# Linear attention and a GELU block on one core: batch 1's preparation reordered between output tiles, and a narrower last store

## The chip, the cores and the metric

The kernel runs on one core of a Trainium2 chip. The metric is the device time of one execution in microseconds, the median over several runs. Profiles are of one execution, taken by the hardware profiler.

## The reference, cut to what matters

```python
# q, k, v: [8 batches, 8 heads, 576 positions, 64], f32
def phi(x): return np.where(x > 0, x, np.exp(x) - 1.0) + 1.0
q_p, k_p = phi(q), phi(k)
kv  = np.einsum('bhsd,bhse->bhde', k_p, v)
z   = np.sum(k_p, axis=2)
num = np.einsum('bhsd,bhde->bhse', q_p, kv)
den = np.einsum('bhsd,bhd->bhs', q_p, z)[..., None] + 1e-06
x   = (num / den) as [4608 tokens, 512]
h   = x @ w_in                       # [512, 2048]
g   = 0.5 * h * (1.0 + np.tanh(c * (h + 0.044715 * h**3)))
out = g @ w_out                      # [2048, 512], f32
```

So each batch is a small linear attention, whose result goes through two large matrix products with a GELU between them.

## The kernel before

**The large products.** Of each batch's 576 positions, 512 ("main") are one iteration `j` of the outer loop; the 64 that are left over from each of the eight batches are gathered into a ninth iteration (`j == B`, 8). An iteration multiplies the transposed attention result `xt` (bf16, 128 partitions x 4 blocks x 512 tokens) by `w_in`: 16 blocks `m` of four 512-column matmuls each (`h_mm`, L349), each block into one PSUM bank, and ScalarE's GELU (L359) takes the bank into `g`. Then four output tiles `t` of 128 tokens are accumulated over 16 matmuls each (`o_mm`, L642), evacuated by ScalarE or VectorE (`evac`, L608) and stored in pairs (L633). A "step" is one h block, or one quarter `u` (four matmuls) of one output tile.

**The order.** The schedule is written out by hand: instructions go to each engine in the order in which the Python code makes them, and each engine takes its own queue strictly in that order. `iteration` walks through the 32 steps ("slots") of an iteration and after each calls `run(j, slot)`, which issues whatever `at(j, slot, ...)` has put there. In iteration 0 the slots 0 to 15 are the h blocks, and 16 to 31 the output steps with `u` outermost: slot 24 is tile 0's third quarter, slot 28 tile 0's last quarter, slots 29, 30 and 31 the last quarters of tiles 1, 2 and 3. So all four output tiles hold a PSUM bank until the end. There are six banks in one rotating pool (`bank`), and one pair of banks (`pair_of_banks`).

**Batch 1's attention** (`plan_second`) lies in those output slots of iteration 0, so that iteration 1 can begin directly after:

- slot 15: phi of q and k (`maps`: ScalarE exponentials, VectorE linear parts and minima, and a part of the w_out cast)
- slot 23: q transposed by TensorE (L469)
- slot 25: v cast to bf16 in two halves (`cast_v_paired`, L241): VectorE one, ScalarE the other
- slot 26: the products `kv` (L263, 72 small matmuls in two halves, the second half on the second half of v), the evacuation into `kvbd` (L290) by VectorE and ScalarE, and the last quarter of w_out's cast (L143) by VectorE, ScalarE and GpSimd
- slots 27 to 30: for each of four chunks `c` of 128 tokens, `n(c)`: four 130-column matmuls (L294) that give numerator and denominator at once, and VectorE's reciprocal and product (`nab_evac`, L307 and L309), which write `x`
- slots 28 to 31: `t(c)`: `x` transposed by TensorE (L341) and copied by ScalarE into `xt` (L342)
- slots 30 and 31: `h_quarter`: the first two h blocks of iteration 1, chunk by chunk, 128 columns at a time

`nab` puts n into the pair of banks, so that the next n has to wait until VectorE has made x from the one before. `nab_in_banks` puts n into two single banks and evacuates them one after the other (L329, L330); the first batch, prepared before the loop, uses the two in turn.

**The first batch** (`first_batch`) also uses `h_quarter`, with three blocks. Batches 2 to 7 are prepared later, from `plan_prepare` and `plan_attention`, with transposes by DMA.

**The output tiles of iteration 0** (`finish`): each is evacuated as soon as its last quarter is issued, tiles 0, 1 and 2 by ScalarE and tile 3 by VectorE; the two stores wait until slot 2 of iteration 1.

**The end.** The last output tile of the ninth iteration (`last_tile`) is made in two halves of 256 columns, each accumulated over all 16 blocks, evacuated (the first by VectorE, the second by ScalarE) and stored in two DMAs of 64 rows, one issued by ScalarE and one by SyncE (`store_rest`, L613).

Of the kernel before, what the change touches and what calls it, by code (L numbers as in the profile page):

```python
# [15 lines left out]
def kernel(  # L16
# [15 lines left out]
    nc = tc.nc  # L32

    B, H, S, D = q.shape
    d_model, d_ff = moe_w_in.shape
    P = 128
    HP = P // 2
    C = 4
    MAIN = P * C
# [34 lines left out]
    def bank(name, shape, dt=FP32):  # L74
        return ps_b.tile(shape, dt, name=name, tag="b")

    def pair_of_banks(name):
        return ps_a.tile([P, 2, 512], FP32, name=name, tag="a")
# [63 lines left out]
    def cast_w_out(i, fn, ms=slice(0, 4)):  # L142
        fn(  # L143
            out=w_out_sb[:, 4 * i + ms.start : 4 * i + ms.stop, :],
            in_=w_st[False, i][:, ms],
        )

    nc.scalar.preload_act_table_set("exp_and_others")
    halves = (slice(0, 2), slice(2, 4))
# [40 lines left out]
    def vp_paired(b):  # L190
        return vps[b % 2].rearrange("p (j u) e -> p j u e", u=NP)
# [48 lines left out]
    def cast_v_paired(b, us, fn):  # L240
        fn(  # L241
            out=vp_paired(b)[:, :, us, 0:D].rearrange("p j u d -> p u j d"),
            in_=ld["v", b][:, us].rearrange("p u (j d) -> p u j d", d=D),
        )
# [72 lines left out]
    def nab(qt_c, b):  # L317
        n_ps = pair_of_banks("n_ps")
        nab_mm(qt_c, kvbds[b % 4], [n_ps[:, a] for a in range(2)])
        return nab_evac(n_ps, b in PAIRED)  # L320
# [23 lines left out]
    xts = {}  # L344
    qts = {}

    def h_mm(h_ps, xt, m, ts=slice(0, MAIN)):
        for c in range(KM):
            nc.tensor.matmul(  # L349
                h_ps[:, ts],  # L350
                lhsT=w_in_sb[:, c, P * m : P * (m + 1)],
                rhs=xt[:, c, ts],
                start=(c == 0),
                stop=(c == KM - 1),
                skip_group_check=True,
            )
# [3 lines left out]

    h_begun = {0: {}, 1: {}}

    def h_quarter(j, c, blocks):
        for m in range(blocks):
            if c == 0:
                h_begun[j][m] = bank("h_ps", [P, MAIN])
            h_mm(h_begun[j][m], xts[j], m, slice(P * c, P * (c + 1)))

    def xt_chunk(j, c):
        return xts[j][:, :, P * c : P * (c + 1)]  # L370
# [1 line left out]
    def gelu_table():  # L372
        nc.scalar.preload_act_table_set("gelu_apprx_tanh_and_others")  # L373
# [65 lines left out]
    fill = {}  # L439

    def at(j, slot, fn, *args):
        j, slot = j + slot // 32, slot % 32
        fill.setdefault((j, slot), []).append((fn, args))

    def run(j, slot):
        for fn, args in fill.get((j, slot), ()):
            fn(*args)

    def plan_second():
        b = 1  # L450
        x = {}

        def maps():
            for n in "qk":
                exp_of(n, b)
            gelu_table()
            for n in "qk":
                linear_of(n, b)
            least_of("q", b)
            cast_w_out(2, nc.vector.tensor_copy, slice(2, 4))  # L460
            least_of("k", b)

        def transpose_q():
            qts[b] = pt.tile([P, C, NP, P], BF16, name="qt")
            for s in range(2):
                t_ps = bank("t_ps", [P, 2, NP, P], BF16)
                for c in range(2):
                    for i in range(NP):
                        nc.tensor.transpose(  # L469
                            t_ps[:, c, i, :],  # L470
                            phi["q", b][:, 2 * s + c, 2 * i : 2 * i + 2, :],
                            ident,
                        )
                nc.scalar.copy(qts[b][:, 2 * s : 2 * s + 2], t_ps)

        def casts():
            cast_v_paired(b, halves[0], nc.vector.tensor_copy)
            cast_v_paired(b, halves[1], nc.scalar.copy)

        def kv():  # L480
            kv_ps = [bank("kv_ps", [P, 2, E]) for _ in range(2)]
            for ii in range(2):
                kv_paired(b, ii, lambda a, ii: kv_ps[a][:, ii, :])
            cast_w_out(3, nc.vector.tensor_copy, slice(0, 1))
            for a, fn in enumerate((nc.vector.tensor_copy, nc.scalar.copy)):
                kv_evac(b, slice(2 * a, 2 * a + 2), kv_ps[a], fn)

        def last_w_out():
            cast_w_out(3, nc.scalar.copy, slice(1, 2))
            cast_w_out(3, nc.gpsimd.tensor_copy, slice(2, 4))  # L490

        def n(c):
            x[c] = nab(qts[b][:, c], b)

        def t(c):
            if c == 0:
                xts[b] = pt.tile([P, NP, MAIN], BF16, name="xt")
            transpose_x(x[c], xt_chunk(b, c), nc.scalar.copy)

        at(0, 15, maps)  # L500
        at(0, 23, transpose_q)
        at(0, 25, casts)
        at(0, 26, kv)
        at(0, 26, last_w_out)
        at(0, 27, n, 0)
        at(0, 28, n, 1)
        at(0, 28, t, 0)
        at(0, 29, n, 2)
        at(0, 29, t, 1)
        at(0, 30, h_quarter, b, 0, 2)  # L510
        at(0, 30, n, 3)
        at(0, 30, t, 2)
        at(0, 31, h_quarter, b, 1, 2)
        at(0, 31, t, 3)
        at(0, 31, h_quarter, b, 2, 2)
        at(0, 31, h_quarter, b, 3, 2)

    def plan_prepare(b, s_linear, s_exp):
        rest = b % 2 == 0
# [87 lines left out]
    def evac(dst, src, on_scalar):  # L607
        (nc.scalar.copy if on_scalar else nc.vector.tensor_copy)(dst, src)  # L608
# [10 lines left out]
    def finish(j, t, o_ps):  # L619
        if j == B:  # L620
            o_sb = pout.tile([P, 2, d_model], FP32, name="o_sb")
            evac(o_sb[:, 0, :], o_ps, t % 2)
            store_rest(t, o_sb, slice(0, d_model), (nc.scalar, nc.sync))
            return
        if t % 2 == 0:
            o_sbs[j, t // 2] = pout.tile([P, 2, d_model], FP32, name="o_sb")
        o_sb = o_sbs[j, t // 2]
        evac(o_sb[:, t % 2, :], o_ps, t < C - 1 if j == 0 else t % 2)
        if t % 2 == 1:
            ov = out[j * S : j * S + MAIN, :].rearrange("(p c) f -> p c f", c=C)[:, t - 1 : t + 1]  # L630

            def store():
                nc.scalar.dma_start(out=ov, in_=o_sb)  # L633

            if j == 0:
                at(1, 2, store)
            else:
                store()

    def o_mm(o_ps, g, t, u, fs=slice(0, d_model)):  # L640
        for m in range(4 * u, 4 * u + 4):
            nc.tensor.matmul(  # L642
                o_ps,
                lhsT=g[:, m, P * t : P * (t + 1)],
                rhs=w_out_sb[:, m, fs],
                start=(m == 0),
                stop=(m == MM - 1),
            )

    def last_tile(g, t):  # L650
        hw = d_model // 2
        o_sb = pout.tile([P, 2, d_model], FP32, name="o_sb")
        for s in range(2):
            fs = slice(hw * s, hw * (s + 1))
            o_ps = bank("o_ps", [P, hw])
            for u in range(4):
                o_mm(o_ps, g, t, u, fs)
            evac(o_sb[:, 0, fs], o_ps, s)
            store_rest(t, o_sb, fs, (nc.scalar, nc.sync))

    def iteration(j):
        xt = xts[j] if j < B else xt_rest
        g = pg.tile([P, MM, MAIN], BF16, name="g")
        hs = [("h", m) for m in range(MM)]
        if j == 0:
            steps = hs + [("o", t, u) for u in range(4) for t in range(C)]
        elif j == 1:
            os = [[("o", t, u) for u in us for t in range(C)] for us in ((0, 1), (2, 3))]
            steps = hs[:8] + os[0] + hs[8:] + os[1]
        else:  # L670
            steps = hs + [("o", t, u) for t in range(C) for u in range(4)]
        o_pss = {}
        for slot, step in enumerate(steps):
            if step[0] == "h":
                m = step[1]
                h_ps = h_begun.get(j, {}).get(m)
                if h_ps is None:
                    h_ps = bank("h_ps", [P, MAIN])
                    h_mm(h_ps, xt, m)
                gelu(g, m, h_ps)  # L680
            else:
                t, u = step[1:]
                if j == B and t == C - 1:
                    if u == 0:
                        last_tile(g, t)
                    continue
                if u == 0:
                    o_pss[t] = bank("o_ps", [P, d_model])
                o_mm(o_pss[t], g, t, u)
                if u == 3:  # L690
                    finish(j, t, o_pss[t])
            run(j, slot)
# [55 lines left out]
```

## Time and profile before

| | us |
|---|---|
| median of 8 runs | 287.89 (287.77 to 288.03) |
| profiled execution | 288.03 |
| its span, first to last instruction | 286.1 |
| TensorE matmuls busy | 276.4 |
| ScalarE busy | 164.8 |
| VectorE busy | 107.7 |
| GpSimd busy | 18.8 |
| granted TensorE clock, mean share | 0.997 |

The profile names engines PE (TensorE), PEld (TensorE's weight loads), DVE (VectorE), ACT (ScalarE), POOL (GpSimd) and SP (SyncE); a "q" behind the name is that engine's issue of a DMA. A row of the timeline has the start in the span, the duration of the group from its first start to its last end, the engine, the line of the kernel, the operation, the tiles it writes and reads, the shape, and the count; in square brackets stands how long the engine was idle before it, and what ended that. Matmuls are pipelined: the end of one is modelled and lies after the start of the next, so that times of a stream of matmuls are read from its starts. A few matmul records are missing in the trace; between 42 and 51 us, one output step is shown with three matmuls in place of four. A line of the DMA issues has the source and the target, the queue, the count, the size of each, and the median time from issue to landing.

### The profile page before, as it was taken

Reading aid. Unit: us, or ns where it says so; the run is one execution under the profiler, and the core shown is the slowest. Engines: PE = TensorE matmul, PEld = TensorE weight load, DVE = VectorE, ACT = ScalarE, POOL = GpSimd, SP = SyncE. Lnnn points to the kernel's source line nnn. Section 1 sums busy time; section 2 is a strip of 40 time slices with the busy share of each in tenths; the row PEclk is TensorE's granted clock in tenths of the full one; section 3 lists DMA queues with packets and bytes.
Section 4 is the critical chain, followed back from the end, with each engine's and each line's share of the span. In section 5 each row is a group of like instructions: output and inputs, shape, how many; then the busy total and the mean of one; then the engine's idle time right before and its main releaser. Section 6 shows DMA issues by size and latency. Waiting matters only on the chain.

```text
span 286.1 us, 4541 instructions
## 1 busy us (share of the span) xinstructions
PE 276.4 (97%) x1839; PEld 137.1 (48%) x1868; DVE 107.7 (38%) x180; ACT 164.8 (58%) x226; POOL 18.8 (7%) x25
## 2 busy tenths in 40 slices
PE   8789999999999999999999999999999999999994
PEld 3464456445455445544554455444544444444443
DVE  3840476534865373544246614640412010000001
ACT  4866886795966934583458635763571275027400
POOL 6066230000000000000000000000000000000000
PEclk9999999999999999999999999999999999999998
DMA  7999999966989958945899489535141210120022
GB/s 249 410 405 398 410 400 283 341 227 188 147 238 315 260 144 206 359 81 147 230 312 174 103 229 360 85 105 152 37 39 49 86 50 0 60 89 1 0 73 73
DMA packets 71379, 53.76 MB, mean 188 GB/s; under 512 B 42048, under 2 KB 62784, under 8 KB 71360
## 3 DMA queue, kind: packets, MB, share of 16 engines
q1 hardware_dynamic: 68656, 44.58, 55.4%
q10 hardware_dynamic: 2704, 8.91, 8.6%
q8 instruction: 14, 0.23, 0.3%
q14 instruction: 5, 0.04, 0.0%
HBM read 36.70 MB, written 9.44 MB: 161 GB/s over the span
## 4 chain that ended last, share of the span: by engine, by line
PE 93%; DMA 3%; DVE 1%; issue 1%; SPq 1%; ACT 0%
PE o_ps L642 43%; PE h_ps L349 43%; PE n_ps L294 3%; DMA v_x<-in_v_dram 3%; PE kv_ps L278 1%; PE t_ps L341 1%; SPq L91 1%; PE kv_ps L263 0%; SPq L96 0%; PE t_ps L469 0%; DVE x L330 0%; DVE vp L241 0%; DVE x L309 0%; ACT xt L342 0%; PE w_ps L382 0%
## 5 line engine op out<-in xcount | busy, mean ns | idle before, releaser
L642 PE MATMUL o_ps<-w_out_sb,g 128*128 128x512 bf16 (+1 forms) x581 | 126.3, 373 | 0.8 <-issue 0.2
L349 PE MATMUL h_ps<-xt,w_in_sb 128*128 128x512 bf16 (+1 forms) x556 | 116.7, 356 | 1.1 <-ACT xt L342 0.2
L359 ACT ACTIVATE g<-h_ps 128x512 bf16<-128x512 f32 x144 | 84.9, 597 | 46.6 <-PE h_ps L349 43.1
L642 PEld LDWEIGHTS <-g 128*128 128x128 bf16 x592 | 57.5, 98 | 65.2 <-issue 0.2
L349 PEld LDWEIGHTS <-w_in_sb 128*128 128x128 bf16 x636 | 57.5, 98 | 59.5 <-issue 0.7
L608 ACT COPY o_sb<-o_ps 128x512 f32<-128x512 f32 (+1 forms) x19 | 10.9, 574 | 61.3 <-PE o_ps L642 54.2
L608 DVE COPY o_sb<-o_ps 128x512 f32<-128x512 f32 (+1 forms) x18 | 12.1, 673 | 69.0 <-PE o_ps L642 69.0
L307 DVE RECIPROCAL r<-n_ps 128x8 f32<-128x8 f32 x34 | 7.0, 207 | 50.4 <-PE n_ps L294 50.4
L309 DVE TENSOR_TENSOR x<-n_ps,r 128x512 bf16<-128x512 f32 x34 | 23.5, 691 | 1.2
L212 ACT ACTIVATE q_e<-q_x 128x2048 bf16<-128x2048 f32 (+1 forms) x9 | 15.5, 1721 | 2.8 <-DMA q_x<-in_q_dram 2.7
L212 ACT ACTIVATE k_e<-k_x 128x2048 bf16<-128x2048 f32 (+2 forms) x9 | 15.8, 1755 | 0.7 <-DMA k_x<-in_k_dram 0.7
L236 DVE TENSOR_TENSOR q_p<-q_p,q_e 128x2048 bf16<-128x2048 bf16 (+1 forms) x9 | 9.9, 1104 | 16.4 <-ACT q_e L212 16.2
L223 DVE TENSOR_SCALAR q_p<-q_x 128x2048 bf16<-128x2048 f32 (+1 forms) x9 | 9.9, 1100 | 14.1 <-DMA q_x<-in_q_dram 14.1
L349 PE MATMUL h_ps<-xt_rest,w_in_sb 128*128 128x512 bf16 x63 | 13.9, 379 | 0.1
L294 PEld LDWEIGHTS <-qt 128*128 128x128 bf16 x128 | 9.7, 98 | 7.2 <-DVE x L309 1.0
L294 PE MATMUL n_ps<-kvbd,qt 128*128 128x130 bf16 x128 | 12.7, 221 | 0.0
L223 DVE TENSOR_SCALAR k_p<-k_x 128x2048 bf16<-128x2048 f32 (+2 forms) x9 | 10.2, 1131 | 5.7 <-DMA k_x<-in_k_dram 5.7
L236 DVE TENSOR_TENSOR k_p<-k_p,k_e 128x2048 bf16<-128x2048 bf16 (+2 forms) x9 | 11.0, 1226 | 0.8 <-ACT k_e L212 0.7
L373 ACT ACT_TABLE_LOAD x8 | 10.3, 1283 | 0.1
L212 ACT ACT_TABLE_LOAD x8 | 10.3, 1283 | 0.1
L382 PE MATMUL w_ps<-warm 128*128 128x512 bf16 x31 | 9.0, 444 | 1.3 <-DVE warm L177 1.2
L290 DVE CAST kvbd<-kv_ps 64x260 bf16<-64x260 f32 (+2 forms) x18 | 6.6, 365 | 8.6 <-PE kv_ps L278 8.2
(49 smaller groups left out, 94.8 us busy)
## 6 DMA issues: line engine op xcount, KB each, us to landing
out_dram<-o_sb ACTq DMA_DIRECT2D x16, 512.0 KB, 3.3
q_x<-in_q_dram SPq DMA_DIRECT2D x6, 1024.0 KB, 7.4
k_x<-in_k_dram SPq DMA_DIRECT2D x6, 1024.0 KB, 11.2
v_x<-in_v_dram SPq DMA_DIRECT2D x6, 1024.0 KB, 6.5
w_st<-in_moe_w_in_dram SPq DMA_DIRECT2D x4, 1024.0 KB, 14.5
w_st<-in_moe_w_out_dram SPq DMA_DIRECT2D x4, 1024.0 KB, 13.6
q_x<-in_q_dram SPq DMA_DIRECT2D x4, 512.0 KB, 8.6
k_x<-in_k_dram SPq DMA_DIRECT2D x2, 576.0 KB, 5.5
```

Of the source, the lines that this page charges most:

```text
L212: nc.scalar.activation(by_chunk(exps[name, b], hs), x[:, hs].rearrange("p h (c d) -> p h c d", d=D), AF.Exp,)
L223: nc.vector.tensor_scalar(by_chunk(phi[name, b], hs), x[:, hs].rearrange("p h (c d) -> p h c d", d=D), 1.0, 1.0, op0=ALU.add, op1=ALU.max,)
L236: nc.vector.tensor_tensor(p, p, e, op=ALU.min)
L294: nc.tensor.matmul(ns[i // 2][rows, 2 * E * (i % 2) : 2 * E * (i % 2 + 1)], lhsT=qt_c[:, i, rows], rhs=kvbd[:, i, :], skip_group_check=True,)
L307: nc.vector.reciprocal(r, n_v[:, :, :, D])
L309: nc.vector.tensor_tensor(x_view(x, paired), n_v[:, :, :, 0:D], r[:, :, :, None].to_broadcast([P, 2, NP, D]), op=ALU.mult,)
L349: nc.tensor.matmul(h_ps[:, ts], lhsT=w_in_sb[:, c, P * m : P * (m + 1)], rhs=xt[:, c, ts], start=(c == 0), stop=(c == KM - 1), skip_group_ ...
L359: nc.scalar.activation(g[:, m, :], h_ps, AF.Gelu_apprx_tanh)
L373: nc.scalar.preload_act_table_set("gelu_apprx_tanh_and_others")
L382: nc.tensor.matmul(w_ps, lhsT=warm[:, 0:P], rhs=warm)
L608: (nc.scalar.copy if on_scalar else nc.vector.tensor_copy)(dst, src)
L642: nc.tensor.matmul(o_ps, lhsT=g[:, m, P * t : P * (t + 1)], rhs=w_out_sb[:, m, fs], start=(m == 0), stop=(m == MM - 1),)
```

## The change

In batch 1's preparation:

- `n(1)` goes into two single banks (`nab_in_banks`), directly behind `n(0)` in slot 27; `n(2)` moves to slot 28, `n(3)` stays in slot 30. The two banks that it takes are those that `kv` had.
- the transposes move later: `t(0)` to slot 29, and `t(1)` and `t(2)` into the middle of slots 30 and 31. These half slots are new: `o_mm` calls `run(j, slot - 0.5)` after the second of its four matmuls.
- only the first h block is begun ahead, in two pieces of 384 and 128 columns at the end of slot 31 (`h_begin`); the second block is made whole, in its own slot.
- output tiles 1 and 2 of iteration 0 are evacuated by ScalarE after the last copy into `xt` (still in slot 31), no longer between those copies.
- half of v's cast goes from ScalarE to GpSimd, ahead of GpSimd's part of the last w_out cast.
- VectorE's part of the last w_out cast goes behind the evacuation of `kv`.

At the end, the last output tile is made in pieces of 256, 128 and 128 columns; ScalarE evacuates the first and the third, VectorE the second.

```diff
+    def h_begin(j, m, ts):
+        if m not in h_begun[j]:
+            h_begun[j][m] = bank("h_ps", [P, MAIN])
+        h_mm(h_begun[j][m], xts[j], m, ts)
+
     def h_quarter(j, c, blocks):
         for m in range(blocks):
-            if c == 0:
-                h_begun[j][m] = bank("h_ps", [P, MAIN])
-            h_mm(h_begun[j][m], xts[j], m, slice(P * c, P * (c + 1)))
+            h_begin(j, m, slice(P * c, P * (c + 1)))
...
         def casts():
             cast_v_paired(b, halves[0], nc.vector.tensor_copy)
-            cast_v_paired(b, halves[1], nc.scalar.copy)
+            cast_v_paired(b, halves[1], nc.gpsimd.tensor_copy)
 
         def kv():
             kv_ps = [bank("kv_ps", [P, 2, E]) for _ in range(2)]
             for ii in range(2):
                 kv_paired(b, ii, lambda a, ii: kv_ps[a][:, ii, :])
-            cast_w_out(3, nc.vector.tensor_copy, slice(0, 1))
             for a, fn in enumerate((nc.vector.tensor_copy, nc.scalar.copy)):
                 kv_evac(b, slice(2 * a, 2 * a + 2), kv_ps[a], fn)
 
         def last_w_out():
+            cast_w_out(3, nc.vector.tensor_copy, slice(0, 1))
             cast_w_out(3, nc.scalar.copy, slice(1, 2))
             cast_w_out(3, nc.gpsimd.tensor_copy, slice(2, 4))
 
         def n(c):
-            x[c] = nab(qts[b][:, c], b)
+            x[c] = (nab_in_banks if c == 1 else nab)(qts[b][:, c], b)
...
         at(0, 27, n, 0)
-        at(0, 28, n, 1)
-        at(0, 28, t, 0)
-        at(0, 29, n, 2)
-        at(0, 29, t, 1)
-        at(0, 30, h_quarter, b, 0, 2)
+        at(0, 27, n, 1)
+        at(0, 28, n, 2)
+        at(0, 29, t, 0)
+        at(0, 29.5, t, 1)
         at(0, 30, n, 3)
-        at(0, 30, t, 2)
-        at(0, 31, h_quarter, b, 1, 2)
+        at(0, 30.5, t, 2)
         at(0, 31, t, 3)
-        at(0, 31, h_quarter, b, 2, 2)
-        at(0, 31, h_quarter, b, 3, 2)
+        at(0, 31, h_begin, b, 0, slice(0, 3 * P))
+        at(0, 31, h_begin, b, 0, slice(3 * P, MAIN))
...
-        evac(o_sb[:, t % 2, :], o_ps, t < C - 1 if j == 0 else t % 2)
+        if j == 0 and t in (1, 2):
+            at(0, 31, evac, o_sb[:, t % 2, :], o_ps, True)
+        else:
+            evac(o_sb[:, t % 2, :], o_ps, t < C - 1 if j == 0 else t % 2)
...
-    def o_mm(o_ps, g, t, u, fs=slice(0, d_model)):
+    def o_mm(o_ps, g, t, u, fs=slice(0, d_model), half=None):
         for m in range(4 * u, 4 * u + 4):
+            if m == 4 * u + 2 and half:
+                run(*half)
             nc.tensor.matmul(
...
     def last_tile(g, t):
-        hw = d_model // 2
         o_sb = pout.tile([P, 2, d_model], FP32, name="o_sb")
-        for s in range(2):
-            fs = slice(hw * s, hw * (s + 1))
-            o_ps = bank("o_ps", [P, hw])
+        for n, fs in enumerate((slice(0, 256), slice(256, 384), slice(384, d_model))):
+            o_ps = bank("o_ps", [P, fs.stop - fs.start])
             for u in range(4):
                 o_mm(o_ps, g, t, u, fs)
-            evac(o_sb[:, 0, fs], o_ps, s)
+            evac(o_sb[:, 0, fs], o_ps, n % 2 == 0)
             store_rest(t, o_sb, fs, (nc.scalar, nc.sync))
...
-                o_mm(o_pss[t], g, t, u)
+                o_mm(o_pss[t], g, t, u, half=(j, slot - 0.5))
```

## The prediction

> **What bounds the kernel now.** I read the page first: busy time and the chain of work that ended last.
>
> ```profile
> PE 276.4 (97%) x1839; PEld 137.1 (48%) x1868; DVE 107.7 (38%) x180; ACT 164.8 (58%) x226; POOL 18.8 (7%) x25
> PE 93%; DMA 3%; DVE 1%; issue 1%; SPq 1%; ACT 0%
> ```
>
> TensorE is the bound: its matmuls are 93% of the chain. No matmul is taken away here, so only TensorE's idle time and the two ends can be won. The waits view gives TensorE hardly any idle time after 51 us, so the edits to batch 1 are worth at most what TensorE idles between 42 and 51 us. Idle time does not show as such there, because a matmul's modelled end overlaps the next start; I take it from starts, in the timeline of TensorE alone (start, duration of the group, operation):
>
> ```profile
> 42.92 0.40 PE L294 MATMUL n_ps<-kvbd,qt 128*128 128x130 bf16 x4
> 43.15 1.15 PE L642 MATMUL o_ps<-w_out_sb,g 128*128 128x512 bf16 x4
> 44.34 0.41 PE L294 MATMUL n_ps<-kvbd,qt 128*128 128x130 bf16 x4
> 44.59 0.38 PE L341 MATMUL t_ps<-ident,x 128*128 128x128 bf16 x4
> 44.81 1.03 PE L642 MATMUL o_ps<-w_out_sb,g 128*128 128x512 bf16 x4
> 45.78 0.41 PE L294 MATMUL n_ps<-kvbd,qt 128*128 128x130 bf16 x4
> ...
> 47.55 0.40 PE L294 MATMUL n_ps<-kvbd,qt 128*128 128x130 bf16 x4
> ...
> 49.32 0.39 PE L341 MATMUL t_ps<-ident,x 128*128 128x128 bf16 x4
> 49.54 0.61 PE L349 MATMUL h_ps<-xt,w_in_sb 128*128 128x128 bf16 x8
> 50.38 0.82 PE L349 MATMUL h_ps<-xt,w_in_sb 128*128 128x128 bf16 x9 [0.23 <-ACT xt L342]
> ```
>
> Undisturbed steps: four 512-column matmuls last 1.03, the last one 0.38 by itself, so they start 0.216 apart (0.86 a step); 128-column ones 0.056 apart (eight in 0.61, one lasts 0.22); a group of n takes 0.24 (42.92 to 43.15), of transposes 0.22 (44.59 to 44.81). Against that, four idle places: the output step at 43.15 lasts 1.15 (0.12 too long: it waits for the ScalarE cast of w_out, which ends at 43.44); it ends at 44.14, n at 44.34 (0.20, for x of chunk 0); the next ends at 45.67, n at 45.78 (0.10, for x of chunk 1); eight matmuls from 49.54 end at 49.99, the next start at 50.38 (0.39, for the copy of xt). Sum **0.81 us**, and no more is there.
>
> The releasers, from the timelines of VectorE and of ScalarE:
>
> ```profile
> 43.35 0.21 DVE L307 RECIPROCAL r<-n_ps 128x8 f32<-128x8 f32 x1 [0.52 <-PE n_ps L294]
> 43.59 0.69 DVE L309 TENSOR_TENSOR x<-n_ps,r 128x512 bf16<-128x512 f32 x1
> ```
>
> ```profile
> 49.74 0.58 ACT L342 COPY xt<-t_ps 128x512 bf16<-128x512 bf16 x1 [0.95 <-PE t_ps L341]
> ```
>
> Two delays follow. n starts at 42.92, its x is ready at 44.28, and the first matmul that waited for it starts at 44.34: 1.42 from n to what needs x. Transposes start at 49.32, their copy ends at 50.32, what needs it starts at 50.38: 1.06.
>
> **The change in batch 1.** I lay the new order out with these steps. n of chunk 0 stays at 42.92. The second n goes into the two banks of kv, whose evacuation the first n has already waited for, so it starts at once, 43.15, and covers what the output step waited for: that runs 43.39 to 44.25, its second matmul due at 43.61 against 43.44. n of chunk 2 needs the pair of banks of chunk 0, hence x of chunk 0: 44.34 (idle 0.09), to 44.59. Output step to 45.45. Transposes 0 to 45.67; two output matmuls to 46.10; transposes 1 to 46.33; two to 46.76; n of chunk 3 to 46.99; two to 47.42; transposes 2 to 47.65; two to 48.08. Transposes 3 need x of chunk 3: 46.76 + 1.42 = 48.18 (idle 0.10). The 384 columns of the first h block need copy 2: 47.42 + 1.06 = 48.48 (idle 0.08); four of them, 0.16 each between the rows of 512 and 256 columns, end at 49.13. The last 128 columns need copy 3: 48.18 + 1.06 = 49.24 (idle 0.11), to 49.46. Block 1 is whole, four times 0.216: 50.33. Before, block 2 began after eight matmuls from 50.38, at 50.83. **Gain 0.50**: some 0.43 of idle time (0.81 - 0.38), and some 0.06 because 32 matmuls of 128 columns become 12 of up to 512.
>
> What hides the rest. VectorE evacuates chunk 1 in halves: in the first batch two reciprocals of 0.17 and two products of 0.42 take 1.10 from first to next, where one of 0.21 and one of 0.69 take some 0.9. x of chunk 1 is then ready at 45.38, needed at 46.10; x of chunk 2 at 46.22, needed at 46.76. Its w_out cast (0.43) moves behind the kvbd casts that end at 42.84: to 43.27 at most, needed at 43.39; without that cover each 0.1 costs 0.1. ScalarE's two output copies (0.58 each) move behind copy 3 (end 49.18): to 50.34, the first gelu to 50.94, where before it ended at about 51.46 (50.86 + 0.60). The banks that these copies free are wanted by h blocks 4 and 5, at 52.05 and 52.92. The store issues keep their place behind the third gelu.
>
> GpSimd takes half of v's cast (ScalarE's 1.18 goes). Its price here is not in the trace; nearest rows, GpSimd's and VectorE's timelines:
>
> ```profile
> 36.51 1.56 POOL L143 CAST w_out_sb<-w_st 128x1024 bf16<-128x1024 f32 x1 [3.59 <-DMA w_st<-in_moe_w_out_dram]
> ```
>
> ```profile
> 36.48 0.69 DVE L143 CAST w_out_sb<-w_st 128x1024 bf16<-128x1024 f32 x1
> 37.09 2.19 DVE L236 TENSOR_TENSOR k_p<-k_p,k_e 128x2304 bf16<-128x2304 bf16 x1
> 39.30 0.76 DVE L241 CAST vp<-v_x 128x1152 bf16<-128x1152 f32 x1
> ```
>
> GpSimd's cast ended at 38.07, and VectorE's product ended 1.2 later though the one of 2048 elements takes 1.22 in all: the two engines took turns. So price the cast as alone (1.89 for 2048 elements, some 1.1 for 1152) behind VectorE's: v lands by 39.28, VectorE to 40.06, GpSimd to 41.2. At the dearest row (1.56 for 1024) it ends at 41.8. It is needed by kv's second half, about 41.33 + 0.36 = 41.69. Cost between 0 and 0.15; I take 0. GpSimd's w_out cast behind it waits for a load that lands at 41.84, as before.
>
> **Later stages.** Loads and exponentials hang on slots and move along with TensorE. What comes at a fixed time (loads issued at 48.28 and 48.80) is first used at 73.5. I let the 0.50 through whole.
>
> **The last tile.** Rows: timeline of the end, and DMA issues on the page.
>
> ```profile
> 278.94 0.69 DVE L608 COPY o_sb<-o_ps 128x512 f32<-128x512 f32 x1 [6.16 <-PE o_ps L642]
> 280.74 0.42 DVE L608 COPY o_sb<-o_ps 128x256 f32<-128x256 f32 x1 [1.11 <-PE o_ps L642]
> 282.43 0.37 ACT L608 COPY o_sb<-o_ps 128x256 f32<-128x256 f32 x1 [6.36 <-PE o_ps L642]
> 282.83 0.50 ACTq L613 DMA_DIRECT2D out_dram<-o_sb  x1
> ```
>
> ```profile
> out_dram<-o_sb ACTq DMA_DIRECT2D x3, 128.0 KB, 2.8
> out_dram<-o_sb ACTq DMA_DIRECT2D x2, 64.0 KB, 2.2
> ```
>
> The tile starts at 278.74 (call it 0). Before: 32 matmuls 0.109 apart, the last starts at 3.38, copy at 3.69 to 4.06, issue at 4.09. After: 16 of those (1.75), then 32 at 0.056: the second part's last starts at 2.59, VectorE's copy at 2.90 takes 0.29 (0.69, 0.42, so 0.13 less per half again), the issue on ScalarE's queue runs 3.22 to 3.72. The third part's last matmul starts at 3.48; ScalarE could copy at 3.74 but is held by that issue until 3.8; copy 0.27 (0.58, 0.37 before it), issue at 4.10. So **nothing is won up to the issue**: the queue's own issue eats the shorter copy. The landing: 64 KB took 2.2 where the 128 KB of the tile before it took 2.6 (the DMA view of that stretch alone); half of that step again gives 0.2. Bounds: 0, and 0.6 if the whole step from 2.8 to 2.2 came again. I take **0.17** for the tail.
>
> A rule speaks against this edit. The Trainium skill, "TensorE: Matmul & The Clock Gate", section "Back-to-back issue gap", puts a stream of weight load and 128-column matmul at about 81 ns each; the row above has 56 ns, and for 512 columns 216 where the page has 131. By the page the 32 narrow ones would end 0.80 later and the change would lose 0.1 in all; by the row nothing. I go by the row, though it has eight in a stream and not 32.
>
> **Sum.** 0.50 + 0.17 = 0.67. The profiled execution took 288.03 (span 286.1), the median of the runs is 287.89; I put the sum on the median: **287.2 us**.
>
> **Rivals.** (1) The forecast, 0.5. (2) The narrow end costs what it gives or more: a matmul stream slower than eight in a row show, or no shorter landing. Then only batch 1 counts: 287.4 to 287.9; for it, one queue that both copies and issues; against it, the 56 ns: 0.2. (3) The wait moves: transposes 3 and both h pieces hang on one chain n, x, transpose, copy, where each link has under 0.12 to spare; another 0.25 late gives 287.5: 0.16. (4) All idle time of the stage goes (0.87) and the landing shrinks by the larger step: 286.6: 0.06. (5) The slower side: GpSimd's cast of a strided half of v is far slower than its casts of weights, or v lands late. kv's second half stands at the head of TensorE's queue, n, outputs and h behind it, and each microsecond after 41.69 is paid in full. It decides from an end at 42.4 (0.7 late, the gain is gone) and is slower from 42.9; with twice the dearest row's rate (3.5 from 40.06, end 43.6) it costs 1.9: 289.1. For it: no such cast in the trace. Against: 1.9 for 2048 elements in every shape shown. 0.08.
>
> Below about 0.2% (0.58 us) the measurement cannot tell from no change. Faster by more: most of (1), (4) and a little of (2): 0.57. Same: 0.36. Slower: 0.07. The range, 286.8 to 287.8, takes in (1), (3), half of (4) and most of (2).
>
> **What would show it.** TensorE's h block 2 starts near 50.3; n of chunk 1 directly behind that of chunk 0; the fourth transposes start about 1.4 after the fourth n; GpSimd's v cast lasts 1.1 to 1.8 and ends before 41.7; 128-column matmuls 0.056 apart in the tile's end; last issue about 4.1 after the tile's start, landing near 2.0. I am wrong if kv waits for GpSimd, if the copies of xt come later than laid out, or if the gain at 51 us is smaller at 268.

## The result, and the profile after

The changed kernel takes 287.21 us, median of 19 runs (287.1 to 287.61); the kernel before, with more runs beside them, 287.95. The ratio is **0.9972, 95% interval 0.9966 to 0.9978**: 0.81 us, between 0.63 and 0.98. The forecast was 287.2. The profiled execution took 287.51, and its span, 285.7, is 0.4 shorter than that of the profiled one of before, although its batch 1 begins 0.30 later: the first load of q landed 0.32 later there. Stretches within one trace are therefore the better measure, and all that follows is compared in that way.

The page of after, the lines that answer to those shown:

```profile
PE 276.9 (97%) x1835; PEld 136.8 (48%) x1864; DVE 107.7 (38%) x182; ACT 163.8 (57%) x226; POOL 19.9 (7%) x26
PE 93%; DMA 3%; DVE 1%; issue 1%; SPq 1%; ACTq 0%; ACT 0%; DVEq 0%
```

TensorE bounds it as before. The timeline of TensorE alone, after (start, duration of the group, operation):

```profile
43.22 0.63 PE L294 MATMUL n_ps<-kvbd,qt 128*128 128x130 bf16 x8
43.69 1.02 PE L650 MATMUL o_ps<-w_out_sb,g 128*128 128x512 bf16 x4
44.65 0.41 PE L294 MATMUL n_ps<-kvbd,qt 128*128 128x130 bf16 x4
44.89 1.02 PE L650 MATMUL o_ps<-w_out_sb,g 128*128 128x512 bf16 x4
45.75 0.39 PE L341 MATMUL t_ps<-ident,x 128*128 128x128 bf16 x4
...
47.06 0.40 PE L294 MATMUL n_ps<-kvbd,qt 128*128 128x130 bf16 x4
...
47.73 0.39 PE L341 MATMUL t_ps<-ident,x 128*128 128x128 bf16 x4
47.95 0.59 PE L650 MATMUL o_ps<-w_out_sb,g 128*128 128x512 bf16 x2
48.49 0.40 PE L341 MATMUL t_ps<-ident,x 128*128 128x128 bf16 x4
48.79 2.45 PE L349 MATMUL h_ps<-xt,w_in_sb 128*128 128x384 bf16 x13
```

Take off the 0.30 by which this trace begins later, and lay it beside the forecast: both n at 42.92 (forecast 42.92 and 43.15, here eight in one group), the output step at 43.39 (43.39), n of chunk 2 at 44.35 (44.34), the fourth n at 46.76 (46.76), the third transposes at 47.43 (47.42), the fourth at 48.19 (48.18), the h block at 48.49 (48.48). What follows the eighth h block shows the gain. The next four rows are of before and of after: the transposes of q, and the first output step of iteration 1.

```profile
37.76 1.06 PE L469 MATMUL t_ps<-ident,q_p 128*128 128x128 bf16 x16
...
56.01 1.24 PE L642 MATMUL o_ps<-w_out_sb,g 128*128 128x512 bf16 x5
```

```profile
38.06 1.06 PE L474 MATMUL t_ps<-ident,q_p 128*128 128x128 bf16 x16
...
55.82 1.46 PE L650 MATMUL o_ps<-w_out_sb,g 128*128 128x512 bf16 x6
```

18.25 before, 17.76 after: **0.49**. With six undisturbed h blocks (5.18) taken off, q's transposes to h block 2 take 13.07 and 12.58; this stretch is called B below. The end, timeline of after, ScalarE and VectorE:

```profile
278.77 0.69 DVE L611 COPY o_sb<-o_ps 128x512 f32<-128x512 f32 x1 [6.16 <-PE o_ps L650]
280.52 0.37 ACT L611 COPY o_sb<-o_ps 128x256 f32<-128x256 f32 x1 [4.62 <-PE o_ps L650]
280.92 1.40 ACTq L616 DMA_DIRECT2D out_dram<-o_sb  x2
281.47 0.29 DVE L611 COPY o_sb<-o_ps 128x128 f32<-128x128 f32 x1 [2.00 <-PE o_ps L650]
282.36 0.27 ACT L611 COPY o_sb<-o_ps 128x128 f32<-128x128 f32 x1 [1.47 <-PE o_ps L650]
282.65 0.52 ACTq L616 DMA_DIRECT2D out_dram<-o_sb  x1
```

And TensorE's narrow matmuls in the same stretch:

```profile
280.48 1.78 PE L650 MATMUL o_ps<-w_out_sb,g 128*128 128x128 bf16 x29
```

The last tile begins 0.20 before the first row of ScalarE and VectorE, at 278.57; the last copy starts 3.79 after that, the issue 4.08 (forecast 3.8 and 4.10), and the landing takes 2.0 in place of 2.2. From the tile's start to the end it is 7.15, and 7.36 before (stretch E): **0.21**.

Between the two stretches, TensorE waits 0.11 at 78 us in after, and 0.09 in before; from there to the last tile both traces take 200.12 at the full granted clock. So the two traces differ by 0.49 - 0.01 + 0.21, about 0.68 from batch 1 on, where the forecast had 0.67 and the times say 0.81, between 0.63 and 0.98.

### The profile page after: what moved, and what is told of

Its sections match the earlier page's. It is cut to its first block, busy times and chain, and to the rows that moved or that the text cites. A ratio compares the mean times of both kernels' runs of the same rounds, so it can differ in the third digit from the quotient of the medians.

```text
span 285.7 us, 4541 instructions
## 1 busy us (share of the span) xinstructions
PE 276.9 (97%) x1835; PEld 136.8 (48%) x1864; DVE 107.7 (38%) x182; ACT 163.8 (57%) x226; POOL 19.9 (7%) x26
## 4 chain that ended last, share of the span: by engine, by line
PE 93%; DMA 3%; DVE 1%; issue 1%; SPq 1%; ACTq 0%; ACT 0%; DVEq 0%
PE h_ps L349 43%; PE o_ps L650 43%; PE n_ps L294 3%; DMA v_x<-in_v_dram 3%; PE kv_ps L278 1%; PE t_ps L341 1%; SPq L91 1%; PE kv_ps L263 0%; SPq L96 0%; PE t_ps L474 0%; DVE x L330 0%; DVE vp L241 0%; DVE x L309 0%; ACTq L616 0%; PE w_ps L385 0%
## 5 line engine op out<-in xcount | busy, mean ns | idle before, releaser
L650 PE MATMUL o_ps<-w_out_sb,g 128*128 128x512 bf16 (+2 forms) x597 | 126.7, 368 | 0.8 <-issue 0.2
L349 PE MATMUL h_ps<-xt,w_in_sb 128*128 128x512 bf16 (+2 forms) x536 | 116.2, 363 | 0.8 <-issue 0.2
L349 PEld LDWEIGHTS <-w_in_sb 128*128 128x128 bf16 x616 | 56.5, 98 | 59.6 <-issue 0.6
L611 ACT COPY o_sb<-o_ps 128x512 f32<-128x512 f32 (+2 forms) x20 | 11.1, 560 | 60.6 <-PE o_ps L650 53.5
L309 DVE TENSOR_TENSOR x<-n_ps,r 128x512 bf16<-128x512 f32 x33 | 22.8, 691 | 1.1
L385 PE MATMUL w_ps<-warm 128*128 128x512 bf16 x31 | 9.8, 473 | 1.3 <-DVE warm L177 1.2
```

Of the source, the lines that this page charges most:

```text
L309: nc.vector.tensor_tensor(x_view(x, paired), n_v[:, :, :, 0:D], r[:, :, :, None].to_broadcast([P, 2, NP, D]), op=ALU.mult,)
L349: nc.tensor.matmul(h_ps[:, ts], lhsT=w_in_sb[:, c, P * m : P * (m + 1)], rhs=xt[:, c, ts], start=(c == 0), stop=(c == KM - 1), skip_group_ ...
L385: nc.tensor.matmul(w_ps, lhsT=warm[:, 0:P], rhs=warm)
L650: nc.tensor.matmul(o_ps, lhsT=g[:, m, P * t : P * (t + 1)], rhs=w_out_sb[:, m, fs], start=(m == 0), stop=(m == MM - 1),)
```

## The experiments

My theory was the sum as forecast: 0.49 from batch 1, because the second n in free banks lets the later order run, and 0.2 from the shorter last landing. The rivals were that the copies or the transposes alone did it, that GpSimd's cast matters, and that the narrow end gives nothing. Results, all from traces except the ratio to before; "idle at 78" is TensorE's wait before the first h block of iteration 2:

| run | B | idle at 78 | E | ratio to before, 95% interval |
|---|---|---|---|---|
| before | 13.07 | 0.09 | 7.36 | |
| after | 12.58 | 0.11 | 7.15 | 0.9972 (0.9966 to 0.9978) |
| e1_stage_only | 12.67 | 0 | 7.37 | 0.9983 (0.9974 to 0.9991) |
| e2_tail_only | 13.07 | 0 | 7.76 | 1.0021 (0.9999 to 1.0044) |
| e3_n1_in_pair | 13.16 | 0.50 | 7.14 | 0.9998 (0.9984 to 1.0012) |
| e4_banks_alone | 13.27 | 0.14 | 7.37 | 1.0013 (1.0004 to 1.0021) |
| e5_copies_between | 12.58 | 0.46 | 7.15 | 0.9969 (0.9956 to 0.9982) |
| e6_v_on_scalar | 12.58 | 0.01 | 7.14 | 0.9962 (0.9947 to 0.9976) |
| e7_gpsimd_thrice | 14.46 | 0 | 7.15 | 1.0046 (1.0022 to 1.0070) |
| e8_earlier | 12.38 | 0 | 7.15 | 0.9958 (0.9940 to 0.9976) |
| e9_tail_same_count | 13.06 | 0.11 | 7.17 | 1.0001 (0.9991 to 1.0011), from another front |
| e10_after_again | 12.58 | 0.32 | 7.15 | 0.9975 (0.9966 to 0.9984) |
| e11_earlier_qr | 12.28 | 0 | 7.13 | 0.9958 (0.9945 to 0.9970) |
| e12_earlier_qr_sync | 12.29 | 0 | 7.23 | 0.9960 (0.9948 to 0.9973) |

In e1 and e8 the casts behind the kv products came 0.12 later than elsewhere, and with them the first n 0.09 later; from the first n on, e1 is like after and e8 0.30 shorter. I have no cause for this delay.

**e1: batch 1's edits without the narrow end.** The last tile in two halves, as in the minus lines of the diff.

> The changed kernel with the last tile made in two halves again, as before; all of batch 1's edits stay. Theory (the two places add up): from the start of batch 1's transposes of q to iteration 1's h block 2 the trace of before has 13.07 us and that of after 12.58; here 12.58, and 7.33 from the last tile's first matmul to the end, as before; in all 0.5 us under before, 287.4. Rival (the tail gives most of the gain, and batch 1's gain is lost later on): less than 0.25 under before.

Measured: 0.49 under before by the ratio (288.26 there), E as before. As the theory had it. In this trace B gives 0.40 of that, and 0.09 comes from the wait at 78 us, which is not there.

**e2: the narrow end without batch 1's edits.**

> The kernel before with the last tile in 256, 128 and 128 columns, nothing else. Theory: 13.07 us from q's transposes to h block 2 as before, 7.12 in place of 7.33 from the last tile's first matmul to the end; in all 0.2 under before, 287.7, at the edge of what can be told from no change. Rival (the narrow pieces give nothing, the 0.21 of the trace is scatter of one execution): 7.33, no difference.

Measured: E is 7.76, longer than before, and the time 0.6 over it, with an interval that just takes in no difference. Neither theory nor rival. The row that is out of place, timeline of ScalarE:

```profile
280.85 0.37 ACT L608 COPY o_sb<-o_ps 128x256 f32<-128x256 f32 x1 [4.62 <-PE o_ps L642]
281.25 2.00 ACTq L613 DMA_DIRECT2D out_dram<-o_sb  x2
283.29 0.27 ACT L608 COPY o_sb<-o_ps 128x128 f32<-128x128 f32 x1 [2.07 <-DMA out_dram<-o_sb]
```

The two issues of the first and second piece reach over 2.00 where after has 1.40, and the last copy waits for them. In the trace the second of them takes 1.13 (0.53 in after), on SyncE at the same time too. The DMA view of that stretch has a row that the view of after has not:

```profile
q8 instruction: 1, 0.02, 2.9%
```

It is a load of 16 KB of instructions that starts at 281.94 and takes 0.92. Stores that were already under way landed later as well: on ScalarE's queue the one of 128 KB took 4.2 in place of 2.6, and that of 64 KB 3.2 in place of 2.2. The loads before it began at 228.4 and 254.8; before and after have none after 260. The narrow end adds 16 matmuls with their weight loads, 32 instructions, to TensorE's stream; batch 1's edits take 40 away.

**e9: the same, with as many TensorE instructions as before.**

```diff
-        keep_warm(18)
+        keep_warm(2)
```

> The kernel before with the narrow last tile and 16 of the first 18 warm-up matmuls left out (they feed no result), so that TensorE has as many instructions as before; its front, and so its whole time, is not to be compared, only the stretch from the last tile's first matmul to the end. In the run with the narrow tile alone that stretch took 7.76 us, a 16 KB instruction load began at 281.94, and the store issues at 282.12 took 1.12 in place of 0.50. Theory (the 32 added instructions made TensorE's stream reach one more load just there): no load after 260 us, issues of 0.5, 7.15 us. Rival (the narrow end itself is slow in the order of before): 7.6 or more again.

Measured: E 7.17, both issues at 0.5, no load after 258.1. The narrow end gives its 0.2 in the old order too, provided that no load falls on it; this is read from the trace, as the time, with another front, doesn't show it. Against e2, the load at 254.8 has moved to 258.1, with a last tile that starts 0.15 earlier: 3.5 later, and the 16 pairs that are left out make 16 times 0.216, also 3.5. So it is TensorE's stream that sets the time of these loads. The Trainium skill, "Runtime: NRT & Kernel Launch", section "Instruction fetch mechanics", says that each engine's instructions come in blocks of 16 KiB, 256 instructions. The distance here comes near it: a weight load and a matmul in 0.216 make 128 pairs 27.6 us, and the last loads in e2 are 26.4 and 27.2 apart.

**e3: the second n back in the pair of banks.**

```diff
-            x[c] = (nab_in_banks if c == 1 else nab)(qts[b][:, c], b)
+            x[c] = nab(qts[b][:, c], b)
...
-        at(0, 27, n, 1)
-        at(0, 28, n, 2)
+        at(0, 28, n, 1)
+        at(0, 29, n, 2)
```

> The changed kernel with the second n back in the pair of banks, in slot 28, the third in slot 29; later transposes, half slots, output copies, GpSimd's cast and the narrow end stay. Theory (the second n in free banks carries the stage's gain, the rest of the order only lets it through): each n then waits 1.42 us from the n before it, 44.34, 45.76, 47.3 in the time of before, and h block 2 comes at 50.87, so 13.1 us from q's transposes, the whole 0.49 gone; in all 0.2 under before, 287.7. Rival (the later transposes and the copies behind them removed the 0.39 at the end by themselves): 12.7 us or less, 287.4 or less.

Measured: B 13.16, the whole 0.49 gone although every other edit stayed; E keeps its 0.2. From the timeline of TensorE, an n that waits for x again, and the first h block of iteration 2:

```profile
46.25 0.41 PE L294 MATMUL n_ps<-kvbd,qt 128*128 128x130 bf16 x4 [0.17 <-DVE x L309]
```

```profile
79.57 1.24 PE L349 MATMUL h_ps<-xt,w_in_sb 128*128 128x512 bf16 x5 [0.34 <-issue]
```

The median is that of before, but the interval takes in the expected 0.2 under it as well, so the time settles nothing here. The profiled execution took 288.62, more than the median of 288.27; TensorE idles 0.50 at 78 us in it (of which more below).

**e4: the second n in two banks, and nothing else.**

```diff
-            x[c] = nab(qts[b][:, c], b)
+            x[c] = (nab_in_banks if c == 1 else nab)(qts[b][:, c], b)
...
-        at(0, 28, n, 1)
+        at(0, 27, n, 1)
```

> The kernel before with one edit: the second n in two single banks, directly behind the first; transposes, h quarters, output copies, v's cast and the last tile as before. Theory (the banks pay only together with later transposes): the first transposes now stand in TensorE's queue for a bank that is free only when x of the first half of chunk 1 is made, some 0.55 later than x of chunk 0, with the output step behind them; h block 2 at 51.0 in the time of before, 13.25 us from q's transposes, 0.2 slower than before, 288.1. Rival (the banks pay by themselves): 12.7 to 12.8 us, 0.3 faster, 287.55.

Measured: B 13.27, 0.20 longer; the time is 0.37 over before by the ratio. The row shows the wait that takes the place of the one removed (timeline of TensorE):

```profile
44.04 1.03 PE L642 MATMUL o_ps<-w_out_sb,g 128*128 128x512 bf16 x4
45.54 0.40 PE L341 MATMUL t_ps<-ident,x 128*128 128x128 bf16 x4 [0.48 <-DVE x L330]
```

The output step ends at 44.90, the transposes start at 45.54, when VectorE has emptied the first of the two borrowed banks (L330). So neither half of the edit pays alone: free banks without later transposes lose 0.2, later transposes without free banks 0.1, and both together win 0.49.

**e5: the output copies back between the copies of xt.**

```diff
-        if j == 0 and t in (1, 2):
-            at(0, 31, evac, o_sb[:, t % 2, :], o_ps, True)
-        else:
-            evac(o_sb[:, t % 2, :], o_ps, t < C - 1 if j == 0 else t % 2)
+        evac(o_sb[:, t % 2, :], o_ps, t < C - 1 if j == 0 else t % 2)
```

> The changed kernel with ScalarE's copies of output tiles 1 and 2 back between the copies of xt. Theory (ScalarE has time for them; the order of the copies is worth next to nothing here): copy 0 of xt comes 0.37 us later and nobody waits, copy 2 0.14 later, copy 3 within 0.02 of where it was; 12.60 us from q's transposes to h block 2 against 12.58, no difference in time. Rival (the 0.39 at the end of the stage went because the output copies got out of the way): 0.3 or more later, 12.9 us, 287.5.

Measured: 12.58, nothing. This edit was worth nothing in this order.

**e6: half of v back on ScalarE.**

```diff
-            cast_v_paired(b, halves[1], nc.gpsimd.tensor_copy)
+            cast_v_paired(b, halves[1], nc.scalar.copy)
```

> The changed kernel with the second half of v cast by ScalarE again. Theory (the cast is off TensorE's path on either engine): the kv products start where they did, 12.58 us from q's transposes to h block 2, no difference in time. Rival (ScalarE's 1.18 us for it were part of what TensorE waited for): 0.1 to 0.4 later.

Measured: 12.58, nothing. Two small edits were not tried alone: the later place of VectorE's w_out cast, and the second h block made whole. In before and in after, the casts into `kvbd` start 4.48 after q's transposes, so the first of them won nothing up to there.

**e7: GpSimd's cast three times.**

```diff
-            cast_v_paired(b, halves[1], nc.gpsimd.tensor_copy)
+            for _ in range(3):
+                cast_v_paired(b, halves[1], nc.gpsimd.tensor_copy)
```

> The changed kernel with GpSimd's half of v's cast made three times over (the same values each time), which delays only its end. Theory: the first waits for VectorE's half, each takes 0.98 us alone as in the trace of after (1.75 with 0.77 beside VectorE), so the last ends at about 43.0 in the time of before, and kv's second half, due at 41.69, waits 1.36 with n, outputs and h behind it: 13.9 us from q's transposes to h block 2, 288.6, paid in full. Rival (the idle 0.39 that is left in the stage takes up part of it): 13.5 to 13.6.

Timelines of VectorE and of GpSimd in after, with the one cast on each:

```profile
39.67 0.77 DVE L241 CAST vp<-v_x 128x1152 bf16<-128x1152 f32 x1
```

```profile
39.70 1.75 POOL L241 CAST vp<-v_x 128x1152 bf16<-128x1152 f32 x1 [1.27 <-DMA v_x<-in_v_dram]
```

Timelines of GpSimd and of TensorE in this run:

```profile
39.40 4.21 POOL L241 CAST vp<-v_x 128x1152 bf16<-128x1152 f32 x3 [1.28 <-DMA v_x<-in_v_dram]
```

```profile
41.49 0.48 PE L263 MATMUL kv_ps<-vp,k_p 64*64 64x65 bf16 x36
43.67 0.48 PE L263 MATMUL kv_ps<-vp,k_p 64*64 64x65 bf16 x36 [1.70 <-POOL vp L241]
```

The casts end at 43.61 and kv's second half starts at 43.67, 1.82 after 41.85, where it was due. B is 1.88 longer than after's, and the time about as much over that of e6, on the same chip. The wait is paid in full, as the theory had it; its size was 1.36 in the expectation, because each further cast takes 1.23 ((4.21 - 1.75) / 2) from start to start, 1.17 by itself, and not 0.98.

**e8: the last chain moved up.**

```diff
-            if m == 4 * u + 2 and half:
-                run(*half)
+            if m >= 4 * u + 2 and half:
+                run(half[0], half[1] + 0.25 * (m - 4 * u - 2))
...
-        at(0, 30, n, 3)
-        at(0, 30.5, t, 2)
-        at(0, 31, t, 3)
+        at(0, 29.5, n, 3)
+        at(0, 30, t, 2)
+        at(0, 30.75, t, 3)
```

> The changed kernel with the last chain moved up: the fourth n directly behind the second transposes, the third transposes at the end of slot 30, the fourth transposes after the third of slot 31's four matmuls. Theory (what is left idle is the chain fourth n, x, transposes, copy of xt): fourth n 0.43 us earlier, its x in time, third copy 0.43 and fourth copy 0.3 earlier, so that the h block runs without a wait; 12.29 us from q's transposes to h block 2 against 12.58, 0.29 under after, 286.9. Rival (x of chunk 2 or a copy becomes late instead): 12.5 or more.

Measured from the first n on: 0.30 shorter than after, as laid out.

**e10 to e12: what is left.** e10 is after itself. e11 is e8 with one more edit, and e12 e11 with another:

```diff
-        at(2 * m - 1, 18, load_rest, "qr", q, m)
+        at(2 * m - 1, 26 if m == 1 else 18, load_rest, "qr", q, m)
```

```diff
-            store_rest(t, o_sb, fs, (nc.scalar, nc.sync))
+            store_rest(t, o_sb, fs, (nc.sync if n == 1 else nc.scalar, nc.sync))
```

> The changed kernel as it is, on the same chip as the next two, to compare them with: 12.58 us from q's transposes to h block 2, 0.1 idle at about 78 us, 7.15 for the end.

> The run with the last chain moved up, and in iteration 1 the load of the second leftover q goes from slot 18 to slot 26, behind the four transposes by DMA that make batch 2's xt. In the trace of after the last of these lands at 78.36 and TensorE's next h block starts at 78.45, 0.11 late; the load stands between them on SyncE's queue for 1.4 us. Theory: the last transposes land 1.0 or more before TensorE asks, no idle there; with the 0.29 of the moved chain, 0.4 under after, 286.8 if after is 287.2. Rival (the transposes wait for something else than the queue): the landing stays within 0.3 of the h block, 0.29 under after or less.

> The kernel just above, and both stores of the last tile's second piece issued by SyncE. Theory (in after, ScalarE's last copy starts at 3.79 us after the tile's start, when the queue has just issued the second piece's store, where TensorE's results would allow 3.74): copy at 3.74, the end 0.05 us earlier, 7.10; hardly to be told in the time. Rival (SyncE's two more issues in a row hold its own last store): 7.2 or more.

SyncE's queue, timelines of e10 and of e11 (issue, duration, operation):

```profile
69.52 1.23 SPq L577 DMA_TRANSPOSE xt<-x  x1
70.80 1.48 SPq L118 DMA_DIRECT2D qr<-in_q_dram  x2
72.54 4.64 SPq L577 DMA_TRANSPOSE xt<-x  x3
77.29 2.51 SPq L544 DMA_TRANSPOSE qt<-q_p  x2
```

```profile
69.24 5.87 SPq L577 DMA_TRANSPOSE xt<-x  x4
76.36 3.81 SPq L544 DMA_TRANSPOSE qt<-q_p  x3
```

and TensorE's, the same two:

```profile
76.79 1.46 PE L650 MATMUL o_ps<-w_out_sb,g 128*128 128x512 bf16 x6
78.41 0.81 PE L349 MATMUL h_ps<-xt,w_in_sb 128*128 128x512 bf16 x3 [0.16 <-issue]
```

```profile
76.30 1.67 PE L650 MATMUL o_ps<-w_out_sb,g 128*128 128x512 bf16 x7
77.81 1.46 PE L349 MATMUL h_ps<-xt,w_in_sb 128*128 128x512 bf16 x6
```

In e10 the last transpose of batch 2's xt lands at 78.32 (2.4 after its issue) and the h block starts at 78.41, 0.32 later than TensorE could. In e11 it lands at 76.25 and TensorE goes on without a pause. The wait differs from trace to trace, and the load's issue with it: in e3, e5 and e10, with 0.50, 0.46 and 0.32 idle, the `qr` row lasts 1.48 to 1.50, in all other traces that have it there 1.28, with 0.14 idle or less.

e11 takes 286.84 against 287.24 of after on the same chip, the expected 0.4 less: it **beats both kernels** (0.9958 against 0.9975 of before; the intervals overlap by a little, but all five runs lie below the fastest of e10's eleven). How much of this comes from moving the load is not shown: e8, without that edit, has the same ratio on another chip, and no idle at 78 in its trace, though there the last transpose lands only 0.18 before TensorE could start.

In e12 the last copy starts at 3.73, as expected, but SyncE now issues three stores in a row:

```profile
280.22 2.61 SPq L616 DMA_DIRECT2D out_dram<-o_sb  x4
```

Its last one goes out 4.41 after the tile's start and not 4.08, and E is 7.23. The rival was right; that edit loses 0.1 at the end, which the times, 286.89 and 286.84, can't confirm.

## Why the prediction was right

- *Batch 1 gives 0.50*: 0.49. The layout from two delays (1.42 from n to what needs x, 1.06 from transposes to what needs the copy) and the undisturbed steps held within 0.02 at each place, and within 0.06 in e3, e4 and e8, which were laid out in the same way (for e8 from the first n on). That the banks and the later transposes need each other was in the layout, though the prediction didn't say it; e3 and e4 showed it.
- *What hides the rest*: shown for the output copies (e5) and for v's cast (e6).
- *GpSimd's cast ends at 41.2, at 41.8 at the dearest row*: 41.15 in the time of before (39.70 + 1.75 - 0.30). The end was right, but not its two parts: alone the cast takes 1.17 (e7) and not 1.1, and beside VectorE's 0.77 it lost 0.58 and not all of it. The slower rival had the right mechanism and price per microsecond (e7), but its condition was 0.5 us away.
- *Nothing won up to the issue, 0.17 by the landing*: the last store is issued 0.01 earlier and lands 0.17 earlier; the other 0.04 of E lies behind the landing. ScalarE's queue did hold its own last copy, 3.79 where 3.74 was possible; e12 shows that moving the issue costs more.
- *128-column matmuls at 56 ns and not the page's 81*: here, 29 in a row last 1.78, one of them 0.22 by itself, so 56 ns apart over the whole stream. The sustained gap of the Trainium skill, "TensorE: Matmul & The Clock Gate", section "Back-to-back issue gap", doesn't hold for this stream; the measurement decides.
- *The 0.50 goes through whole, since loads and exponentials hang on slots*: the sum held (0.47 is left at the last tile), but the step failed. It left out the transposes by DMA: TensorE waited 0.09 for their landing in before, 0.11 in after, and 0.32 and 0.50 in other runs. That the two traces compared here have nearly the same wait is luck; against e10, the same kernel, only 0.26 of the 0.49 would be left. The wait passed unseen because the prediction took starts up to 51 us only and trusted the waits view behind it. That view doesn't list the 0.09 and the 0.11, which lie under the modelled end of the matmul before, and puts e10's 0.32 at 0.16, as "issue". The row to look at was SyncE's queue, where a load that isn't urgent stood ahead of three transposes.
- *Instruction loads* were in no step. The full change has 8 instructions fewer on TensorE than before, and none fell on its end; with the narrow end alone one did, and cost 0.6. As the prediction hadn't looked at them, that is luck too.
- *No matmul is taken away* is not so: 32 of 128 columns become 12 of up to 512, which the prediction counts further on, as 0.06.
- That 287.21 meets 287.2 to the last digit is chance: the interval of the gain is 0.35 wide.

## What to carry to other kernels

Lay the new order out by hand, from starts, undisturbed steps and the few delays from issue to use. Here this was right to 0.02 us at each step, close enough to say which edits need each other. A buffer that is borrowed to remove one wait must be followed to the next instruction that wants it. Where a gain is to pass through later stages, look at every transfer that lands just ahead of its use, also where the waits view doesn't name it: take TensorE's idle time from starts there too.

## What the runs showed of the hardware

- A load of 16 KB of instructions (0.92 us) that fell among stores made the issue of two of them take 1.13 in place of 0.5, one on each queue, the landing of one already under way 4.2 in place of 2.6, and the end 0.6 longer (e2); 32 instructions more on TensorE decided whether it fell there (e9).
- GpSimd's cast of 1152 elements took 1.17 with VectorE idle (e7), and 1.75 beside VectorE's cast of 0.77 (after).
- The landing of a store of 64 rows, from its issue, fell from 2.6 (128 KB) to 2.2 (64 KB) and 2.0 (32 KB) on ScalarE's queue (after).
- The load of a leftover q (two issues) ahead of three transposes by DMA took 1.28 on SyncE's queue in nine traces, and TensorE waited for the transposes 0.14 or less; in e3, e5 and e10 it took 1.48 to 1.50, and TensorE waited 0.32 to 0.50.
